# Chunk bounds of a selective attention: from zero-padded blocks on four 64x64 array tiles to full heads on eight 64x32 tiles

## The chip, the cores and the metric

The kernel runs on one core of a Trainium2 chip. The metric is the device time of one execution in microseconds (us); here it is the median of three. A core has five engines with instruction streams of their own: TensorE (PE: matmuls, and PEld: the loading of their weights), VectorE (DVE), ScalarE (ACT), GpSimd (POOL), and SyncE (SP), which only issues transfers here. They work at the same time and wait for each other through semaphores.

## The reference

Two parts, run one after the other: an attention over a selection of chunks, and a gated feed-forward network (FFN).

```python
# q, k, v: 4 batches, 8 heads, 768 positions, 64 dimensions (float32)
chunk, nc, top_k = 32, 24, 6
k_min, k_max = min and max of k over each chunk of 32 positions      # per dimension
ub = sum over d of max(q*k_min, q*k_max)          # bound of each query against each chunk
ub = where(causal by chunks, ub, -1e9)
top_chunks = the 6 chunks of the largest ub, for each query
scores = q @ k.T / 8, kept only in the chosen chunks and not after the query
attn_out = softmax(scores) @ v
x = attn_out as [3072, 512]
xn = x / rms(x) * rms_g
out = (silu(xn @ w_gate) * (xn @ w_val)) @ w_out          # 512 -> 1536 -> 512
```

The change touches `ub` alone. The kernel uses that max(q*k_min, q*k_max) = q*k_min + relu(q)*(k_max - k_min), since k_max is at least k_min: the sum over d becomes two matmuls, q against k_min and relu(q) against the difference.

## The kernel before

One Python program plans the whole kernel: each operation is entered with its engine (or several engines it may go to), a duration, a priority and its dependencies, and a list scheduler fixes the order on every engine before the program is built. So a change of one operation can move all others. TensorE, like the others, then takes its instructions in that fixed order. The sequence is cut into 12 blocks of 256 queries (4 batches by 3), each in two groups `g` of 4 heads; `m` is the block's place in its batch. In the blocks with m = 0 only the last 64 queries need a selection (`w = 64`), as the others see 6 chunks or fewer.

Queries and keys are turned in 32x32 squares, so in `qT` and `kT` the partitions hold 4 heads x 32 dimensions, and the two halves `h` of the 64 dimensions lie side by side in the free dimension. A head's 64 dimensions are then on no common set of 64 partitions. Before, the block `BD` makes up for that: on 64 partitions it has two heads, 32 dimensions each, and its 64 columns belong to one head or the other, with zeros where head and column don't match (`own` is the pattern of ones and zeros). Four matmuls (`t`: two halves of the dimensions, times k_min and difference) add up one bound:

```python
        def upper():
            for k_, g in enumerate(gs):
                qT, qr = sides[i, g][0:2]
                qs = [at(qT)[:, :, BLK - w:], qr()]
                qs = [x.rearrange("p h (j c r) -> p h j c r", c=2, r=CH) for x in qs]
                d = BD[b, g]
                for t in range(4):
                    for hp in range(2):
                        for c in range(2):
                            TE.matmul(bank()[hp][64 * c:64 * (c + 1), k_],
                                      d[64 * hp:64 * (hp + 1), t, :],
                                      qs[t // 2][64 * hp:64 * (hp + 1), t % 2, :, c, :],
                                      start=(t == 0), stop=(t == 3),
                                      skip_group_check=True)

```

Its inputs are made per block and group of heads:

```python
        turn("k")
        half("k")
        for n, op in enumerate((ALU.min, ALU.max)):
            plan.op(f"ext{n}{J}", "DVE", 0.585, 0.67, lambda n=n, op=op: VE.tensor_reduce(
                out=at(kx)[:, n], in_=at(kT).rearrange("p h (c t) -> p h c t", t=CH),
                axis=AXX, op=op), base + 1, reads=[kT], writes=[kx],
                takes=[(kx, "kx")] if n == 0 else ())
        def sub(eng):
            return lambda: eng.tensor_tensor(
                out=at(kx)[:, 1], in0=at(kx)[:, 1], in1=at(kx)[:, 0], op=ALU.subtract)

        first_dk.append(flex(f"dk{J}", {"POOL": (0.175, 0.22, sub(GE)), "DVE": (0.1, 0.16, sub(VE))},
                             base + 2, reads=[kx], writes=[kx]))
        for n in range(2):
            def place(eng, n=n):
                return lambda: eng.tensor_tensor(
                    out=BD[b, g].rearrange("p t (h c) -> p t h c", h=2)[
                        :, 2 * n:2 * n + 2, :, CB * m:CB * (m + 1)],
                    in0=at(kx)[:, n].unsqueeze(2).to_broadcast([P, 2, 2, CB]),
                    in1=own[:].unsqueeze(1).to_broadcast([P, 2, 2, CB]), op=ALU.mult)

            flex(f"bd{n}{J}", {"POOL": (0.21, 0.255, place(GE)), "DVE": (0.11, 0.17, place(VE))},
                 base + 2, reads=[kx, "own", bd], writes=[bd, bd + (m,)])
        turn("q")
        half("q")
        qR = ("qR", *J)

        def qr():
            return at(qraw)[:, g].rearrange("p j h d -> p (j h d)")[:, 0:2 * w].rearrange(
                "p (h s) -> p h s", h=2)

        def relu(eng):
            return lambda: eng.tensor_scalar(
                out=qr(), in0=at(qT)[:, :, BLK - w:], scalar1=HUGE, scalar2=0.0,
                op0=ALU.min, op1=ALU.max)

        flex(f"relu{J}", {"POOL": (0.58 if m else 0.25, 0.62 if m else 0.29, relu(GE)),
                          "DVE": (0.34 if m else 0.14, 0.42 if m else 0.22, relu(VE))},
             base + 2, reads=[qT, qraw], writes=[qR])

        sides[i, g] = (qT, qr, bd, qR, qraw)
```

`turn` is a VectorE transpose, `half` a cast to bf16 for the score matmuls (GpSimd or ScalarE), `flex` an operation that may go to any of the engines named. GpSimd takes `place` or `relu` where the planner finds room there. After `upper`, VectorE turns the bounds back, finds the six largest (`max`), compares and turns the result into masks, which are added to the scores on TensorE.

The FFN's gate works in pieces of 512 columns: two matmul groups into PSUM (`wg`, `wv`), tanh on ScalarE, `tg` on VectorE, and the product `hh` either on GpSimd from a ScalarE copy of the second result (`vs`), or directly on VectorE (the set `DIRECT`). While TensorE would wait in the first 60 us of the plan, dummy matmuls keep it busy (`keep_busy`).

Of the kernel before, what the change touches and what calls it, by code (L numbers as in the profile page):

```python
# [8 lines left out]
FP32 = mybir.dt.float32  # L9
BF16 = mybir.dt.bfloat16  # L10
ALU = mybir.AluOpType
# [103 lines left out]
class Plan:  # L115

    SHARES = ("scale", "relu", "bd0", "bd1", "dk", "mk")
    PATIENT = {"DVE": 0.6}  # L120
    STICK = 60
    RESERVED = ("hh",)
# [188 lines left out]
def kernel(  # L311
# [50 lines left out]
    buffers("VX", 19, [P, 2, 4, D + 1], BF16)  # L362
    buffers("qb", 5, [P, 2, BLK], BF16)
    buffers("kx", 3, [P, 2, 2, CB], FP32)
    buffers("ubn", 1, [P, NG, 2, 4, CH], FP32)
# [18 lines left out]
    pat = sb.tile([P, CH], BF16, name="pat")  # L384
    own = sb.tile([P, 2, CB], FP32, name="own")
    chunkrow = sb.tile([P, S], BF16, name="chunkrow")
# [9 lines left out]
    wo = sb.tile([P, NHT, DM], BF16, name="wo")  # L396
    BD = {(b, g): sb.tile([P, 4, 64], FP32, name=f"BD{b}{g}") for b in range(B) for g in range(NG)}
    TH = DFF // 3
# [5 lines left out]
    assert sorted(ORDER) == [(b, m) for b in range(B) for m in range(NBLK)]  # L404
    PACE, LEAD = 23.0, 60
    MARGIN = 2.0
    FIRST = 8
    FROM = 3
    GATES = {"0": "dk(0, 0, 0)", "1": "dk(0, 0, 0)", "2": "dk(0, 0, 0)", "o": "dk(0, 0, 0)"}
    SPLIT = {0, 1}  # L410
    APART = {0}
    BYDMA = set(range(FROM, len(ORDER)))
    PACKED = {0, 1, 2}
    DIRECT = {(i, hp) for i in range(len(ORDER)) for hp in range(KH) if i >= 8 and hp % 2}

# [3 lines left out]
    def due_attn(i):  # L419
        return PACE * i - LEAD  # L420
# [27 lines left out]
    def constants():  # L448
        def warm():
            SE.activation(out=mhalf[0:1, 0:1], in_=eps6[0:1, 0:1], func=ACT.Exp)  # L450

        plan.op("eps", "POOL", 0.04, 0.1, lambda: GE.memset(eps6[:], 1.0e-6), -400, writes=["eps"])
        plan.op("table", "ACT", 1.4, 1.7, warm, -400, reads=["eps"], writes=["tab"])
        plan.op("half", "POOL", 0.04, 0.12, lambda: GE.memset(mhalf[:], -0.5), -200,
                reads=["tab"], writes=["half"])
        plan.op("ident", "POOL", 0.95, 1.0, lambda: masks.make_identity(nc, ident[:]), -390,
                writes=["ident"])
        plan.op("own", "DVE", 0.2, 0.3, lambda: VE.tensor_reduce(
            out=own[:, :, 0], in_=ident.rearrange("p (x h c) -> p h x c", h=2, c=CH),
            axis=AXXY, op=ALU.add), -380, reads=["ident"], writes=["own0"])  # L460
        plan.op("own8", "DVE", 0.1, 0.2, lambda: VE.tensor_copy(
            own[:, :, 1:CB], own[:, :, 0:1].to_broadcast([P, 2, CB - 1])), -379,
            reads=["own0"], writes=["own0", "own"])
        plan.op("pat", "DVE", 0.2, 0.3, lambda: VE.tensor_reduce(
            out=pat[:], in_=ident.rearrange("p (a c) -> p c a", c=CH), axis=AXX, op=ALU.max),
            -378, reads=["ident"], writes=["pat"])
        plan.op("chunkrow", "DVE", 0.8, 0.9, lambda: VE.tensor_scalar(
            out=chunkrow.rearrange("p (c t) -> p c t", t=CH),
            in0=pat[:, 0:S // CH].unsqueeze(2).to_broadcast([P, S // CH, CH]),
            scalar1=MASKED, scalar2=None, op0=ALU.mult), -300, reads=["pat"], writes=["chunkrow"])  # L470
        for i, (key, t) in enumerate(BD.items()):
            plan.op(f"BD0{key}", "POOL", 0.25, 0.33, lambda t=t: GE.memset(t[:], 0.0), -370 + 42 * i,
                    writes=[("BD", *key)])
        for i, t in enumerate(store["VX"]):
            plan.op(f"ones{i}", "POOL", 0.035, 0.14, lambda t=t: GE.memset(t[:, :, :, D:D + 1], 1.0),
                    -300 + i, writes=[("ones", i)])
# [4 lines left out]

    HELD = {2: (("wg", 1), ("wg", 1)), 3: (("wo", 1), ("wo", 1))}

# [25 lines left out]
    def loads_due(i, n):  # L509
        return -500 + 10 * i + n if i < 2 else due_attn(i) - 20 + n  # L510

# [20 lines left out]

    first_dk = []


    sides = {}

    def pick(i, gs):
# [21 lines left out]
        def upper():  # L560
            for k_, g in enumerate(gs):
                qT, qr = sides[i, g][0:2]
                qs = [at(qT)[:, :, BLK - w:], qr()]
                qs = [x.rearrange("p h (j c r) -> p h j c r", c=2, r=CH) for x in qs]
                d = BD[b, g]
                for t in range(4):
                    for hp in range(2):
                        for c in range(2):
                            TE.matmul(bank()[hp][64 * c:64 * (c + 1), k_],  # L569
                                      d[64 * hp:64 * (hp + 1), t, :],  # L570
                                      qs[t // 2][64 * hp:64 * (hp + 1), t % 2, :, c, :],
                                      start=(t == 0), stop=(t == 3),
                                      skip_group_check=True)

        reads = []
        for g in gs:
            qT, qr, bd, qR, qraw = sides[i, g]
            reads += [bd] + [bd + (x,) for x in range(m + 1)] + [qT, qR, qraw]
        o = plan.op(f"upper{tag}", "PE", (0.925 if m else 0.49) * n, (0.925 if m else 0.49) * n + 0.165,
                    upper, base + 3, reads=reads, writes=ub, takes=[(x, "F") for x in ub])  # L580
# [56 lines left out]
    def job(i, g):  # L637
# [34 lines left out]
        def sub(eng):  # L672
# [4 lines left out]
                             base + 2, reads=[kx], writes=[kx]))  # L677
        for n in range(2):
            def place(eng, n=n):
                return lambda: eng.tensor_tensor(  # L680
                    out=BD[b, g].rearrange("p t (h c) -> p t h c", h=2)[
                        :, 2 * n:2 * n + 2, :, CB * m:CB * (m + 1)],
                    in0=at(kx)[:, n].unsqueeze(2).to_broadcast([P, 2, 2, CB]),
                    in1=own[:].unsqueeze(1).to_broadcast([P, 2, 2, CB]), op=ALU.mult)

            flex(f"bd{n}{J}", {"POOL": (0.21, 0.255, place(GE)), "DVE": (0.11, 0.17, place(VE))},
                 base + 2, reads=[kx, "own", bd], writes=[bd, bd + (m,)])
        turn("q")
        half("q")
        qR = ("qR", *J)  # L690

# [4 lines left out]
        def relu(eng):  # L696
            return lambda: eng.tensor_scalar(  # L697
                out=qr(), in0=at(qT)[:, :, BLK - w:], scalar1=HUGE, scalar2=0.0,
                op0=ALU.min, op1=ALU.max)

        flex(f"relu{J}", {"POOL": (0.58 if m else 0.25, 0.62 if m else 0.29, relu(GE)),
                          "DVE": (0.34 if m else 0.14, 0.42 if m else 0.22, relu(VE))},
             base + 2, reads=[qT, qraw], writes=[qR])

        sides[i, g] = (qT, qr, bd, qR, qraw)
        yield
# [89 lines left out]
        for s in range(2):  # L796
# [13 lines left out]

            pri = base + (-4 if i in SPLIT and not s else 6)
            have = list(pts.values()) + [(pts[x], "ab"[s] if i in SPLIT and x == m else "")
# [95 lines left out]
    def ffn(i):  # L908
# [6 lines left out]
        for toks, h0 in pieces:  # L915
# [10 lines left out]
            for nm, p_, w in (("wg", gp, wg), ("wv", vp, wv)):  # L926
# [11 lines left out]
            plan.op(f"tanh{U}.{hp}", "ACT", 0.48, 0.6, lambda th=th, gp=gp: SE.activation(  # L938
                out=at(th), in_=at(gp), func=ACT.Tanh, scale=0.5), pri - 10, reads=[gp], writes=[th],
                takes=[(th, "th")])  # L940
# [4 lines left out]
            if (i, h0 // 2) in DIRECT:  # L945
                plan.op(f"hh{U}.{hp}", "DVE", 0.6, 0.69, lambda tg=tg, vp=vp, hh=hh: VE.tensor_tensor(
                    out=at(hh), in0=at(tg), in1=at(vp), op=ALU.mult), pri - 60, reads=[tg, vp],
                    writes=[hh], takes=[(hh, "hh")])
                continue
# [3 lines left out]
            plan.op(f"hh{U}.{hp}", "POOL", 1.11, 1.16, lambda tg=tg, vs=vs, hh=hh: GE.tensor_tensor(  # L953
                out=at(hh), in0=at(tg), in1=at(vs), op=ALU.mult), pri - 40, reads=[tg, vs],
                writes=[hh], takes=[(hh, "hh")])
        for s in whole:
# [8 lines left out]
            def project(h0, h1, s=s, op=op, part=part):  # L965
                for ht in range(h0, h1):
# [5 lines left out]
            hhs = sorted({part(ht)[0] for ht in range(last)}, key=str)  # L972
            pri = base + 10 + s
            o = plan.op(f"project{i}.{s}", "PE", 0.216 * last, 0.216 * last + 0.17,
# [4 lines left out]
            o = plan.op(f"project{i}.{s}+", "PE", 0.216 * 2, 0.216 * 2 + 0.17,  # L979
                        lambda project=project: project(last, NHT), pri - 30,  # L980
                        reads=[part(NHT - 1)[0], op], writes=[op])
# [61 lines left out]

    for o in plan.run(in_order=("kraw", "qraw", "vraw", "kT", "qT", "kb", "qb", "VX", "xsT", "xs", "hh", "xnat"),
                      fill=(1.6, 5.6, 60.0, 0.0565, 0.216, "F", keep_busy)):
        o.fn()
# [29 lines left out]
```

## Time and profile before

The three runs took 303.33, 303.45 and 303.48 us; the median is 303.45. The profiled execution has a span of 302.1 us with the TensorE clock granted in full (0.999).

| What | Number | Where |
|---|---|---|
| bound matmuls, line L569 | 768 records, 219 to 320 ns each | groups by line |
| of these, 64x128 and 64x32 | 512 and 256 records | groups by form |
| gate and value matmuls, L931 | 1216 records | groups by line |
| `BD` placement, L680 | 26 on GpSimd, 22 on VectorE | groups by line |
| `mk`, `mtd`, `ubn` (selection) on VectorE | 792, 712, 422 ns for a whole block | groups by form |
| `hh` products, L953 and L946 | 60 on GpSimd at 1197 ns, 12 on VectorE at 688 ns | groups by form |
| DMA | 33.24 MB, mean 110 GB/s | page, part 2 |

The durations of matmul records overlap, since they are pipelined and several array tiles run at once: what a run of matmuls costs is read from the starts in the timeline. The page's slices give busy shares in tenths for 40 equal parts of the span; the stretches give busy us of PE, PEld, DVE, ACT and POOL in a window. A group's row reads: line, engine, operation, output and input, shape, count | busy us, mean ns of one | idle time before it and what ended it.

### The profile page before, as it was taken

To read this page: it belongs to the slowest core of one execution; us is meant where nothing else is said; L and a number is where in the kernel's file an instruction comes from. 1 tells how busy PE (TensorE), PEld (TensorE's weight loads), DVE (VectorE), ACT (ScalarE), POOL (GpSimd) and SP (SyncE) were. 2 spreads that over 40 slices of the span, in tenths; PEclk is the share of its full clock that TensorE was granted. 3 is DMA by queue.
4 is the path that set the end of the run, shared out by engine and by line. 5 is a ranking of instruction groups with operands and counts; after the bars stand their busy time and mean duration, and the time that the engine had idled before them with its cause. 6 is when DMAs were issued, how large, how long until landed. Compare 5 with 4: busy or idle time off the path is not lost.

```text
span 302.1 us, 11334 instructions
## 1 busy us (share of the span) xinstructions
PE 288.5 (96%) x4643; PEld 219.6 (73%) x4668; DVE 220.7 (73%) x564; ACT 213.2 (71%) x371; POOL 162.0 (54%) x273
## 2 busy tenths in 40 slices
PE   8799999999999999999989999999999999999994
PEld 8456786758758858876876788587678588588671
DVE  5997995978897899999999999296254256267250
ACT  3486975879659888987976798568777597554240
POOL 5695675758747684682767578239334044033130
PEclk9999999999999999999999999999999999999999
DMA  7999995758575764666674610101120011020101
GB/s 188 229 201 229 238 215 122 190 117 208 88 167 147 161 142 135 146 110 158 153 159 101 171 37 7 69 4 37 37 69 4 35 53 24 28 61 20 71 0 69
DMA packets 84771, 33.24 MB, mean 110 GB/s; under 512 B 75376, under 2 KB 79984, under 8 KB 84720
## 3 DMA queue, kind: packets, MB, share of 16 engines
q1 hardware_dynamic: 79120, 27.28, 38.5%
q0 software_dynamic: 4752, 4.72, 9.3%
q8 instruction: 36, 0.59, 0.8%
q10 hardware_dynamic: 848, 0.53, 0.7%
q14 instruction: 15, 0.12, 0.1%
HBM read 28.58 MB, written 6.29 MB: 115 GB/s over the span
## 4 chain that ended last, share of the span: by engine, by line
PE 72%; DVE 9%; DMA 7%; ACT 4%; issue 3%; SPq 2%; POOL 1%; ACTq 0%; DVEq 0%; POOLq 0%
PE F L931 33%; PE F L968 18%; PE S L731 6%; PE F L807 6%; PE F L569 5%; DMA wv<-in_moe_w_val_dram 3%; DVE xs L861 3%; DMA qraw<-in_q_dram 2%; PE S L742 2%; SPq L429 2%; DVE tg L942 2%; PE F L1042 1%; DVE kx L668 1%; ACT junk L843 1%; DVE qT L653 1%
## 5 line engine op out<-in xcount | busy, mean ns | idle before, releaser
L781 ACT ACTIVATE pt<-S 128x1024 bf16<-128x1024 f32 (+3 forms) x104 | 87.0, 861 | 17.0 <-PE S L742 16.2
L953 POOL TENSOR_TENSOR hh<-tg,vs 128x512 bf16<-128x512 bf16 x60 | 71.5, 1197 | 45.4 <-ACT vs L950 32.6
L931 PE MATMUL F<-xsT,wg 128*128 128x256 bf16 (+1 forms) x608 | 74.8, 267 | 2.4 <-DVE tg L942 1.9
L931 PE MATMUL F<-xsT,wv 128*128 128x256 bf16 (+1 forms) x608 | 74.7, 267 | 0.9 <-DVE tg L942 0.5
L942 DVE SCALAR_TENSOR_TENSOR tg<-th,F 128x512 bf16<-128x512 bf16 x72 | 48.9, 681 | 31.0 <-ACT th L938 30.2
L968 PE MATMUL F<-wo,hh 128*128 128x512 bf16 x268 | 65.3, 379 | 1.3 <-POOL BD L680 0.2
L931 PEld LDWEIGHTS <-wg 128*128 128x128 bf16 x608 | 55.7, 98 | 10.6 <-issue 3.4
L931 PEld LDWEIGHTS <-wv 128*128 128x128 bf16 x608 | 55.1, 98 | 9.3 <-issue 1.5
L938 ACT ACTIVATE th<-F 128x512 bf16<-128x512 f32 x72 | 43.1, 600 | 20.2 <-PE F L931 19.4
L751 POOL TENSOR_SCALAR_AFFINE_SELECT pt<-pt 128x512 bf16<-128x512 bf16 x48 | 31.5, 661 | 36.9 <-ACT pt L781 36.3
L968 PEld LDWEIGHTS <-hh 128*128 128x128 bf16 x288 | 27.0, 98 | 28.8 <-POOL qraw L697 0.2
L950 ACT ACTIVATE vs<-F 128x512 bf16<-128x512 f32 x60 | 35.7, 603 | 9.1 <-PE F L931 6.5
L731 PE MATMUL S<-qb,kb 32*128 32x256 bf16 (+1 forms) x800 | 33.2, 253 | 1.7 <-ACT qb L660 1.4
L668 DVE TENSOR_REDUCE kx<-kT 128x16 f32<-128x512 f32 x48 | 30.1, 665 | 0.0
L807 PEld LDWEIGHTS <-pt 128*128 128x128 bf16 x672 | 24.8, 98 | 4.8 <-issue 0.8
L807 PE MATMUL F<-VX,pt 128*128 128x65 bf16 x672 | 27.2, 194 | 0.6 <-DVE ubn L599 0.4
L731 PEld LDWEIGHTS <-kb 32*128 32x128 bf16 x800 | 14.2, 92 | 15.0 <-issue 14.1
L861 DVE SCALAR_TENSOR_TENSOR xs<-xnat,ri_all,gB 128x512 bf16<-128x512 bf16 x18 | 21.1, 1212 | 2.7 <-POOL ri_all L851 2.7
L984 ACT ACTIVATE osb<-F 128x512 f32<-128x512 f32 x15 | 8.7, 593 | 18.1 <-PE F L968 18.1
L826 DVE TENSOR_TENSOR xnat<-F,rden 128x256 bf16<-128x256 f32 x48 | 20.0, 423 | 1.2
L742 PE MATMUL S<-mtd,chunkrow 32*128 32x128 bf16 (+2 forms) x384 | 20.8, 203 | 0.0
L742 PE MATMUL S<-mto,chunkrow 32*128 32x128 bf16 (+2 forms) x384 | 20.4, 203 | 0.0
(62 smaller groups left out, 340.2 us busy)
## 6 DMA issues: line engine op xcount, KB each, us to landing
vraw<-in_v_dram SPq DMA_DIRECT2D x24, 256.0 KB, 4.2
out_dram<-osb SPq DMA_DIRECT2D x24, 256.0 KB, 2.3
kraw<-in_k_dram SPq DMA_DIRECT2D x72, 64.0 KB, 2.5
qraw<-in_q_dram SPq DMA_DIRECT2D x72, 64.0 KB, 2.2
wg<-in_moe_w_gate_dram POOLq DMA_DIRECT2D x3, 512.0 KB, 10.1
wv<-in_moe_w_val_dram POOLq DMA_DIRECT2D x3, 512.0 KB, 11.8
wo<-in_moe_w_out_dram POOLq DMA_DIRECT2D x3, 512.0 KB, 20.7
kraw<-in_k_dram SPq DMA_DIRECT2D x10, 128.0 KB, 4.6
```

Of the source, the lines that this page charges most:

```text
L668: plan.op(f"ext{n}{J}", "DVE", 0.585, 0.67, lambda n=n, op=op: VE.tensor_reduce(out=at(kx)[:, n], in_=at(kT).rearrange("p h (c t) -> p h c ...
L731: TE.matmul(s[a // 2][:, a % 2, c0:c0 + q1 - q0], kbt[r, t, ks], qbt[r, t, q0:q1], start=(t == 0), stop=(t == 1 and not mask), skip_group_ ...
L742: TE.matmul(o, chunkrow[r, BLK * kg + P * e:BLK * kg + P * (e + 1)], mv, start=False, stop=(d == 1), skip_group_check=True)
L751: GE.affine_select(out=d, in_=d, compare_op=ALU.is_ge, fill=0.0, base=0, pattern=[[0, 4], [1, P]], channel_multiplier=-1)
L781: lambda pt=pt, hs=hs, c0=c0, c1=c1, x=sc[hp]: SE.activation(out=at(pt)[:, hs, c0:c1], in_=at(x)[:, :, c0:c1], func=ACT.Exp, scale=SCALE), ...
L807: TE.matmul(o[:, a, :], p_[:, a, off:off + P], vt[:, e, a, :], start=(kb_ == 0 and a == 0), stop=(kb_ == nkb - 1 and a == 3), skip_group_c ...
L931: TE.matmul(at(p_)[:, n * W:(n + 1) * W], w[:, g, ht * P:(ht + 1) * P], at(xT)[:, g, x0:x0 + W], start=(g == 0), stop=(g == NP - 1), skip_ ...
L938: plan.op(f"tanh{U}.{hp}", "ACT", 0.48, 0.6, lambda th=th, gp=gp: SE.activation(out=at(th), in_=at(gp), func=ACT.Tanh, scale=0.5), pri - 1 ...
L942: VE.scalar_tensor_tensor(out=at(tg), in0=at(th), scalar=1.0, in1=at(gp), op0=ALU.add, op1=ALU.mult), pri - 20, reads=[th, gp], writes=[tg ...
L950: plan.op(f"vcopy{U}.{hp}", "ACT", 0.48, 0.6, lambda vs=vs, vp=vp: SE.activation(out=at(vs), in_=at(vp), func=ACT.Copy), pri + 0.1, reads= ...
L953: plan.op(f"hh{U}.{hp}", "POOL", 1.11, 1.16, lambda tg=tg, vs=vs, hh=hh: GE.tensor_tensor(out=at(hh), in0=at(tg), in1=at(vs), op=ALU.mult) ...
L968: TE.matmul(at(op)[:], at(key)[:, o:o + P], wo[:, ht, :], start=(ht == 0), stop=(ht == NHT - 1))
```

## The change

Now `BD` is [128, 2, 2, 32] instead of [128, 4, 64]: 64 partitions hold all 64 dimensions of one head, for k_min and the difference (`n_`) and for two heads (`p_`). There are no zeros to multiply. A matmul has 64 rows and 32 columns (24 of them chunks), and the eight of one `n_` go to eight different tiles of the array: 2 row groups (`e`) by 4 column groups. To have the dimensions on the rows, half of each 128 partitions must move by 32: for the bounds by four small VectorE copies after one whole copy; for q by a whole copy into a new float32 buffer `QX` and four copies of 32 partitions each, on VectorE or ScalarE. The relu then reads `QX`. So four matmuls with half zeros become two without, for each head and query half, and the number of matmuls stays the same, as each now serves one head and not two.

The planner's settings change as well: the pace and lead of attention before the FFN (23 to 24, 60 to 67), how long VectorE may wait for a more urgent operation (0.6 to 0.3), how strongly TensorE stays in one tile mode (60 to 25), some priorities; the direct `hh` product is allowed from block 5 on and not 8; blocks 3 and 4 send their FFN input over TensorE instead of a transposing DMA (`FROM`); block 1 selects its two groups of heads apart (`APART`).

```diff
-    SHARES = ("scale", "relu", "bd0", "bd1", "dk", "mk")
-    PATIENT = {"DVE": 0.6}
-    STICK = 60
+    SHARES = ("qx", "qm", "scale", "relu", "bd0", "bd1", "dk", "mk")
+    PATIENT = {"DVE": 0.3}
+    STICK = 25
...
+    buffers("QX", 3, [P, 2, BLK], FP32)
...
-    BD = {(b, g): sb.tile([P, 4, 64], FP32, name=f"BD{b}{g}") for b in range(B) for g in range(NG)}
+    BD = {(b, g): sb.tile([P, 2, 2, 32], FP32, name=f"BD{b}{g}") for b in range(B) for g in range(NG)}
...
-    PACE, LEAD = 23.0, 60
+    PACE, LEAD = 24.0, 67
...
-    FROM = 3
+    FROM = 5
...
-    APART = {0}
+    APART = {0, 1}
...
-    DIRECT = {(i, hp) for i in range(len(ORDER)) for hp in range(KH) if i >= 8 and hp % 2}
+    DIRECT = {(i, hp) for i in range(len(ORDER)) for hp in range(KH) if i >= 5 and hp % 2}
...
+    CROSS = [(0, 32, 0, 1), (64, 96, 0, 1), (32, 0, 1, 0), (96, 64, 1, 0)]
...
-                for t in range(4):
-                    for hp in range(2):
+                for n_ in range(2):
+                    for p_ in range(2):
                         for c in range(2):
-                            TE.matmul(bank()[hp][64 * c:64 * (c + 1), k_],
-                                      d[64 * hp:64 * (hp + 1), t, :],
-                                      qs[t // 2][64 * hp:64 * (hp + 1), t % 2, :, c, :],
-                                      start=(t == 0), stop=(t == 3),
-                                      skip_group_check=True)
+                            for e in range(2):
+                                r = slice(64 * e, 64 * (e + 1))
+                                x = 64 * c + 32 * p_
+                                TE.matmul(bank()[e][x:x + 32, k_], BD[b, g][r, n_, p_, :],
+                                          qs[n_][r, p_, :, c, :], start=(n_ == 0), stop=(n_ == 1),
+                                          skip_group_check=True)
...
-        for n in range(2):
-            def place(eng, n=n):
...
-            flex(f"bd{n}{J}", {"POOL": (0.21, 0.255, place(GE)), "DVE": (0.11, 0.17, place(VE))},
-                 base + 2, reads=[kx, "own", bd], writes=[bd, bd + (m,)])
+        def place(eng):
+            def go():
+                new = BD[b, g][:, :, :, CB * m:CB * (m + 1)]
+                eng.tensor_copy(new, at(kx))
+                for lo, hi, p_, t in CROSS:
+                    VE.tensor_copy(new[hi:hi + 32, :, p_], at(kx)[lo:lo + 32, :, t])
+            return go
+
+        plan.op(f"bd{J}", "DVE", 0.34, 0.4, place(VE), base + 2, reads=[kx, bd], writes=[bd, bd + (m,)])
...
+        flex(f"qx{J}", {"DVE": (0.34 if m else 0.14, 0.42 if m else 0.22, spread(VE)),
+                        "POOL": (0.58 if m else 0.25, 0.62 if m else 0.29, spread(GE)),
+                        "ACT": (0.54 if m else 0.24, 0.63 if m else 0.33, spread(SE))},
+             base + 2, reads=[qT], writes=[qx], takes=[(qx, "QX")])
+        for n in range(2):
+            def move(eng, n=n):
+                def go():
+                    for lo, hi, p_, t in CROSS[2 * n:2 * n + 2]:
+                        o, x = at(qx)[hi:hi + 32, p_, BLK - w:], at(qT)[lo:lo + 32, t, BLK - w:]
+                        if eng is SE:
+                            SE.activation(out=o, in_=x, func=ACT.Copy)
+                        else:
+                            eng.tensor_copy(o, x)
+                return go
+
+            flex(f"qm{n}{J}", {"DVE": (0.39 if m else 0.19, 0.47 if m else 0.27, move(VE)),
+                               "ACT": (0.8 if m else 0.54, 0.9 if m else 0.62, move(SE))},
+                 base + 2, reads=[qT, qx], writes=[qx + (n,)])
...
         def relu(eng):
             return lambda: eng.tensor_scalar(
-                out=qr(), in0=at(qT)[:, :, BLK - w:], scalar1=HUGE, scalar2=0.0,
+                out=qr(), in0=at(qx)[:, :, BLK - w:], scalar1=HUGE, scalar2=0.0,
```

`SHARES` lists how the names of those VectorE operations begin that the planner keeps apart in time from GpSimd's. The new operation is named `bd(...)`, which no entry matches.

## The prediction

> **What bounds the kernel now.** I read the page's busy shares first, then its slices. Each digit of a slice is a tenth of 7.6 us.
>
> ```profile
> PE 288.5 (96%) x4643; PEld 219.6 (73%) x4668; DVE 220.7 (73%) x564; ACT 213.2 (71%) x371; POOL 162.0 (54%) x273
> ...
> PE   8799999999999999999989999999999999999994
> ...
> DVE  5997995978897899999999999296254256267250
> ACT  3486975879659888987976798568777597554240
> ```
>
> TensorE is near full from the third slice on. That alone isn't proof, because up to 60 us the kernel fills waiting time with dummy matmuls (41 of 128x512 and 86 of 128x128 by the table of groups), and they count as busy. So I asked for the stretches after 60 us: columns are stretch, length, then busy us of PE, PEld, DVE, ACT, POOL.
>
> ```profile
> 100.00:120.00 20.00, 19.57 (x363) 14.79 (x364) 19.22 (x68) 17.24 (x29) 12.59 (x22) 1.00 0.62 140
> 120.00:140.00 20.00, 19.79 (x333) 14.98 (x334) 18.58 (x52) 17.11 (x30) 11.59 (x17) 1.00 0.58 117
> 140.00:160.00 20.00, 18.92 (x374) 16.12 (x370) 19.37 (x51) 17.10 (x30) 14.29 (x22) 1.00 0.70 167
> 160.00:180.00 20.00, 19.65 (x384) 15.17 (x387) 19.35 (x67) 15.72 (x27) 13.40 (x23) 1.00 0.46 108
> ...
> 240.00:260.00 20.00, 19.89 (x356) 16.12 (x356) 10.66 (x19) 15.62 (x25) 7.12 (x9) 1.00 0.15 42
> ```
>
> Two things are to be seen. PE is the bound everywhere after 60 us, with about 2 us idle in 100 to 180. But in those 80 us VectorE has only 80 - 76.5 = 3.5 us left: it is a second bound lying right under the first. After 200 us (attention over, only the FFN left) VectorE is half free.
>
> Next, the matmuls that change, line L569, in the timeline of one group with 256 queries (start, length, count):
>
> ```profile
> 97.05 0.67 PE L569 MATMUL F<-qT,BD 64*64 64x128 f32 x16
> 97.54 0.62 PE L569 MATMUL F<-qraw,BD 64*64 64x128 f32 x16
> 97.97 0.62 PE L569 MATMUL F<-qT,BD 64*64 64x128 f32 x16
> 98.41 0.62 PE L569 MATMUL F<-qraw,BD 64*64 64x128 f32 x16
> 98.96 1.07 PE L807 MATMUL F<-VX,pt 128*128 128x65 bf16 x28
> ```
>
> Starts, not lengths, give the cost: 98.96 - 97.05 = 1.91 us for 64 records. A float32 matmul leaves two records, so these are the 32 matmuls of two head groups. Sixteen records take 0.43 us, and on 4 tiles that is 4 per tile at 108 ns each. The small groups (64 queries) take 1.07 us:
>
> ```profile
> 63.28 0.43 PE L569 MATMUL F<-qT,BD 64*64 64x32 f32 x16
> ...
> 64.35 0.62 PE L887 MATMUL F<-ident,xs 128*128 128x128 bf16 x8
> ```
>
> There are 8 large groups and the equivalent of 4 small ones: 8 x 1.91 + 4 x 1.07 = 19.6 us of TensorE in all.
>
> [...] 108 ns per record and tile with no gap. No run here shows 8 yet. [...] placing the bounds (L680) on VectorE takes 143 ns at best, 179 in the median, and 1030 at worst. [...] The one-source relu here (128x512, three on VectorE) averages 574 ns with a median over both sizes of 412[...].
>
> **The change part by part.**
>
> *TensorE.* The number of matmuls stays (384), and so does what each streams. What changes is that eight run at once. 64 records on 8 tiles are 8 per tile x 108 ns = 0.86, plus the ramp of the first sixteen (0.49 against 0.43) and some tail: 0.95 us against 1.91. Over 8 large groups that saves 8 x 0.95 = **7.6 us**, all after 60 us, where PE is the bound. A small group should come to 0.5 to 0.6 us, but three of the four stand before 60 us, where dummy matmuls still take up slack; I count **0.5 us**. The instruction order of the changed program (built, not timed) has 16 more TensorE transposes, as two more blocks take that way to the FFN instead of a DMA: eight of them take 0.55 us on the chain, so +**1.1 us**. It has 126 stretches of tile mode against 122, which I leave at zero. Sum on TensorE: -7.0 us.
>
> *VectorE.* Gone: 22 placements (22 x 298 ns = 6.6), 4 differences (4 x 435 = 1.7), 4 weighted scalings (4 x 1212 = 4.8), the `own` pattern (1.7). New: 24 copies of 128x32 and 96 of 32x16 into BD. No row of before has such copies; a memset of 64x16 takes 72 ns, so I estimate 75 to 100 ns: 24 x 0.1 + 96 x 0.075 = 9.6. Then 16 q moves at some 0.2 and 6 at 0.1 (3.8), five more relus (+2.0), 9 more direct products `hh` (9 x 688 = 6.2), 7 more output evictions (7 x 682 = 4.8), 1.5 of smaller pieces. Net 27.9 - 14.8 = **+13 us**[...].
>
> ```profile
> L680 DVE TENSOR_TENSOR BD<-kx,own 128x32 f32<-128x32 f32 x22 | 5.8, 298 | 0.0
> ...
> L673 DVE TENSOR_TENSOR kx<-kx 128x16 f32<-128x16 f32 x7 | 3.0, 435 | 0.0
> ...
> L628 ACT ACTIVATE mto<-mtd 64x256 bf16<-64x256 bf16 x5 | 2.1, 416 | 3.0 <-DVE mtd L618 2.9
> ...
> L628 ACT ACTIVATE mto<-mtd 64x64 bf16<-64x64 bf16 x1 | 0.3, 255 | 0.0
> ```
>
> *ScalarE.* It gets 74 of the 96 q moves. The nearest rows are the `mto` copies above: 48 x 416 + 26 x 255 = 26.6 us, plus 8 whole-q copies (about 4.7), 4 scalings and 8 evictions of transposed x (6.3). It loses 9 `vs`, 7 `osb`, 15 casts and 2 V casts at 593 to 643 ns (19.2). Net **+18 us**, to some 77% of the span; in 100 to 180 us it was 84% busy.
>
> *GpSimd.* It loses 26 placements (6.8) and 9 products (9 x 1197 = 10.8), and gains 13 casts (8.7) and 16 whole-q copies (7.6): about -2 us.
>
> *On the path.* VectorE had 3.5 us left in 100 to 180. The part of its new work that belongs to attention (BD, moves and relus less placements and differences) is 9.6 + 3.8 + 2.0 - 8.3 = 7 us over 24 jobs, about 4 of it in that stretch, plus part of the direct products. FFN work can slide to the half-empty end, but TensorE takes its matmuls in a fixed order, so a late selection stops it. I add **+2 us** of new TensorE waits there. 303.45 - 7.0 + 2.0 gives **298.4 us**.
>
> **Rivals.** (1) *TensorE gain in full*: the order was replanned (pace 24, lead 67, attention further ahead), and VectorE's added work falls where it has room, in the first 60 us (80% busy) and after 200. For it: PE hardly waits for VectorE today (2.4 us for `tg` in all). It makes 295 to 297. (2) *VectorE becomes the bound*: the new BD copies come five in a row[...], and the placements already average twice their best case. If each set of five loses 0.3 to 0.4 us, that is 8 us more, and the whole gain is gone: 302 to 305. Against it: `dk` moves to GpSimd and the copies are short. (3) *Eight tiles don't run at twice four*: weight loads or issue set a floor. For it: the small group takes 1.07 us although its stream is a quarter, so something else than streaming already costs 67 ns per matmul and tile. Against it: its weights halve too, 64 to 32 columns. If a large group only reaches 1.3 us, the gain falls to 4.9 us, and the time to about 301. (4) *ScalarE holds up the exponentials*, whose S buffers gate the score matmuls: 1 to 3 us; its 16% of slack speaks against more.
>
> **Range and chances.** Rivals 1 and 2 span 295 to 305; I hold full success and partial loss about equally likely, total loss less so, as the plan was retuned around the new loads. 80% range 293.5 to 303.5. The 2% line lies at 297.4, just under my centre: faster 0.42, same 0.52, slower 0.06.
>
> **What would show it.** In the profile after: a large group of L569's successor with 64 records in 0.95 us between starts (right), or 1.3 and more (rival 3). PE busy down by about 7 us, DVE up to about 234 to 240, ACT to about 230. BD copies near 75 to 100 ns (right) or several hundred (rival 2). PE idle in 60 to 200 us, 2.9 us now, at 5 to 6 (right), under 4 (rival 1), or over 9 with VectorE as releaser (rival 2). The prediction would fail if the retimed order, and not the costs listed, moved the time: for instance a later start of the FFN, or a longer tail after 280 us.

## The result, and the profile after

The changed kernel takes 329.26 us against 303.47 us: slower by a factor of 1.0856 (95% interval 1.0818 to 1.0893). The prediction was 298.4 us, with 293.5 to 303.5 as its range. So it was wrong, and by far.

First the page of the changed kernel: the engines' busy time, then the slices (the last row is the granted TensorE clock in tenths).

```profile
PE 297.6 (91%) x4681; PEld 220.5 (67%) x4681; DVE 259.2 (79%) x702; ACT 232.0 (71%) x434; POOL 159.0 (48%) x268
...
PE   8798858989699899699979989899999999999995
...
DVE  6979996497989999989999999998985436427361
...
PEclk9879997997969999879999999999999999999999
```

ScalarE gained 18.8 us and GpSimd lost 3.0, as predicted (18 and -2). VectorE gained 38.5 us where 13 were expected, or some 19 at most (a busy time of up to 240 us). Its stretch of nines now lasts until about 220 us, and TensorE has gaps all through it. The granted TensorE clock, full before (0.999), drops in several slices of the first half, in one to 0.6.

The stretches show the same. The first fence is after; columns as before: stretch, length, busy us of PE, PEld, DVE, ACT, POOL, then the granted clock.

```profile
100.00:120.00 20.00, 18.13 (x295) 13.26 (x294) 19.17 (x72) 16.94 (x32) 12.97 (x20) 1.00 0.42 104
120.00:140.00 20.00, 17.00 (x265) 12.07 (x263) 19.52 (x42) 17.92 (x33) 14.03 (x24) 0.93 0.43 91
140.00:160.00 20.00, 20.00 (x346) 15.48 (x345) 18.73 (x56) 17.25 (x33) 14.28 (x19) 0.90 0.63 145
160.00:180.00 20.00, 17.82 (x416) 13.87 (x400) 19.27 (x75) 15.30 (x27) 8.25 (x13) 1.00 0.61 127
180.00:200.00 20.00, 18.03 (x277) 13.20 (x276) 19.30 (x43) 16.25 (x29) 12.01 (x21) 1.00 0.46 112
```

VectorE is as full as before in 100 to 180 us, and stays so in 180 to 220 as well, where it was two thirds busy at 180 to 200. Of the first 80 us here, TensorE is idle for 7 and not 2. Over the whole stretch 60 to 200 us, one row of each kernel, before and then after:

```profile
60.00:200.00 140.00, 137.12 (x2454) 105.47 (x2463) 123.03 (x363) 111.18 (x190) 87.91 (x139) 1.00 0.54 123
```

```profile
60.00:200.00 140.00, 125.78 (x2023) 91.46 (x2021) 129.47 (x367) 111.43 (x207) 83.06 (x128) 0.94 0.49 115
```

TensorE idles 14.2 us instead of 2.9 and gets through 2023 records instead of 2454. The prediction had set "over 9 with VectorE as releaser" as the sign of its second rival. The releasers, from the view of TensorE's waits (us in total, times, longest):

```profile
PE F L949 <- DVE tg L960: 3.6, 4, 2.0
PE F L949 <- DVE xnat L844: 2.8, 1, 2.8
PE F L825 <- DVE xsT L918: 2.6, 1, 2.6
PE F L905 <- DVE tg L960: 2.2, 1, 2.2
PE F L566 <- DVE BD L678: 2.1, 5, 1.1
```

These are the five with the largest totals. All are VectorE's, but four are not the changed operations: it looks as if VectorE were late as a whole, and with it whatever stands next in its queue. The chain that ended last agrees. Its shares of the span by engine, before and then after:

```profile
PE 72%; DVE 9%; DMA 7%; ACT 4%; issue 3%; SPq 2%; POOL 1%; ACTq 0%; DVEq 0%; POOLq 0%
```

```profile
PE 43%; DVE 35%; DMA 11%; issue 4%; SPq 3%; POOL 2%; ACT 1%; DVEq 0%; ACTq 0%; POOLq 0%
```

What made it late should show in VectorE's groups, where new rows stand (count | busy us, mean ns):

```profile
L678 DVE COPY BD<-kx 32x16 f32<-32x16 f32 x96 | 28.8, 300 | 1.9
...
L703 DVE COPY QX<-qT 32x256 f32<-32x256 f32 x16 | 5.7, 354 | 0.3
L676 DVE COPY BD<-kx 128x32 f32<-128x32 f32 x24 | 5.2, 219 | 0.2
L703 DVE COPY QX<-qT 32x64 f32<-32x64 f32 x6 | 2.9, 482 | 0.1
```

A copy of 16 elements per partition takes 300 ns in the mean, and the 120 bound copies take 34.0 us where 9.6 were estimated. The line's own view gives minimum, median and maximum:

```profile
L678 DVE COPY BD<-kx x96: 161/169/1336, 11.5 to 224.5; 32x16 f32<-32x16 f32 x96
```

So two things are too dear: the floor of 161 ns, twice the estimate, and a tail up to 1336. One place in the timeline shows both. VectorE, then GpSimd (start us, length us):

```profile
107.91 0.14 DVE L676 COPY BD<-kx 128x32 f32<-128x32 f32 x1
108.08 1.82 DVE L678 COPY BD<-kx 32x16 f32<-32x16 f32 x4
109.93 0.59 DVE L676 COPY BD<-kx 128x32 f32<-128x32 f32 x1
110.55 0.70 DVE L678 COPY BD<-kx 32x16 f32<-32x16 f32 x4
```

```profile
108.11 0.61 POOL L656 CAST qb<-qT 128x512 bf16<-128x512 f32 x1 [0.45 <-DVE BD L676]
108.67 0.62 POOL L689 COPY QX<-qT 128x512 f32<-128x512 f32 x1
109.26 0.61 POOL L715 TENSOR_SCALAR qraw<-QX 128x512 f32<-128x512 f32 x1
109.84 0.65 POOL L769 TENSOR_SCALAR_AFFINE_SELECT pt<-pt 128x512 bf16<-128x512 bf16 x1
111.27 0.64 POOL L769 TENSOR_SCALAR_AFFINE_SELECT pt<-pt 128x512 bf16<-128x512 bf16 x1 [0.79 <-ACT pt L799]
```

While GpSimd works without a break (108.1 to 110.5), four copies need 1.82 us. Record by record, the first takes 165 ns and the next three 495, 542 and 578, and each of these three ends 21 to 27 ns after one of GpSimd's operations does. In the pause that follows, four need 0.70. Of the 96 copies, 31 took over 200 ns. All of these began while a GpSimd operation ran (as did 14 of the other 65), and 28 of them ended within 40 ns after the end of one.

The part that the change was made for did come. A large group of bound matmuls, 64 records, in TensorE's timeline:

```profile
238.99 0.45 PE L566 MATMUL F<-QX,BD 64*32 64x128 f32 x16
239.23 0.42 PE L566 MATMUL F<-qraw,BD 64*32 64x128 f32 x16
239.45 0.48 PE L566 MATMUL F<-QX,BD 64*32 64x128 f32 x16
239.67 0.52 PE L566 MATMUL F<-qraw,BD 64*32 64x128 f32 x16
240.13 2.12 PE L986 MATMUL F<-wo,hh 128*128 128x512 bf16 x9
```

Sixteen records start every 0.22 us and not every 0.43: eight tiles do run at twice four. The group takes 240.13 - 238.99 = 1.14 us against 1.91. Six of the eight large groups ran without a break: five at the full clock, in 1.09 to 1.44 us (the longest with a wait of 0.24 behind it), and one in 1.61 us, mostly at a granted clock of 0.50. The small group (64 queries) that ran whole at the full clock took 0.84 us against 1.07.

### The profile page after: what moved, and what is told of

It reads as the page before. It is cut to its first block, busy times and chain, and to the rows that moved or that the text cites. A ratio compares the mean times of both kernels' runs of the same rounds, so it can differ in the third digit from the quotient of the medians.

```text
span 328.4 us, 11559 instructions
## 1 busy us (share of the span) xinstructions
PE 297.6 (91%) x4681; PEld 220.5 (67%) x4681; DVE 259.2 (79%) x702; ACT 232.0 (71%) x434; POOL 159.0 (48%) x268
## 4 chain that ended last, share of the span: by engine, by line
PE 43%; DVE 35%; DMA 11%; issue 4%; SPq 3%; POOL 2%; ACT 1%; DVEq 0%; ACTq 0%; POOLq 0%
PE F L949 23%; PE F L986 10%; DVE kx L663 6%; DVE BD L678 5%; DMA kraw<-in_k_dram 4%; DMA vraw<-in_v_dram 4%; DVE tg L960 4%; PE F L825 4%; DVE qT L648 3%; SPq L429 3%; PE S L749 3%; DVE kT L648 3%; PE F L566 2%; DVE xnat L844 2%; DVE m L603 1%
## 5 line engine op out<-in xcount | busy, mean ns | idle before, releaser
L971 POOL TENSOR_TENSOR hh<-tg,vs 128x512 bf16<-128x512 bf16 x51 | 60.2, 1182 | 66.7 <-ACT vs L968 35.7
L949 PE MATMUL F<-xsT,wg 128*128 128x256 bf16 (+1 forms) x608 | 78.2, 275 | 9.9 <-DVE tg L960 3.4
L949 PE MATMUL F<-xsT,wv 128*128 128x256 bf16 (+1 forms) x608 | 77.4, 273 | 0.2 <-DVE tg L960 0.2
L960 DVE SCALAR_TENSOR_TENSOR tg<-th,F 128x512 bf16<-128x512 bf16 x72 | 48.4, 678 | 25.8 <-ACT th L956 25.2
L986 PE MATMUL F<-wo,hh 128*128 128x512 bf16 x288 | 68.7, 384 | 0.0
L949 PEld LDWEIGHTS <-wv 128*128 128x128 bf16 x608 | 57.0, 100 | 8.5 <-issue 0.8
L968 ACT ACTIVATE vs<-F 128x512 bf16<-128x512 f32 x51 | 30.4, 601 | 8.0 <-PE F L949 6.9
L678 DVE COPY BD<-kx 32x16 f32<-32x16 f32 x96 | 28.8, 300 | 1.9
L701 ACT ACTIVATE QX<-qT 32x256 f32<-32x256 f32 (+1 forms) x74 | 26.5, 358 | 2.5 <-POOL QX L689 1.3
L1004 DVE TENSOR_SCALAR osb<-F 128x512 f32<-128x512 f32 x16 | 10.8, 681 | 15.6 <-PE F L986 15.5
L861 ACT ACTIVATE junk<-xnat 128x512 bf16<-128x512 bf16 x24 | 15.1, 628 | 11.1 <-DVE xnat L844 10.8
```

The source lines that it names most:

```text
L678: VE.tensor_copy(new[hi:hi + 32, :, p_], at(kx)[lo:lo + 32, :, t])
L949: TE.matmul(at(p_)[:, n * W:(n + 1) * W], w[:, g, ht * P:(ht + 1) * P], at(xT)[:, g, x0:x0 + W], start=(g == 0), stop=(g == NP - 1), skip_ ...
L960: VE.scalar_tensor_tensor(out=at(tg), in0=at(th), scalar=1.0, in1=at(gp), op0=ALU.add, op1=ALU.mult), pri - 20, reads=[th, gp], writes=[tg ...
L968: plan.op(f"vcopy{U}.{hp}", "ACT", 0.48, 0.6, lambda vs=vs, vp=vp: SE.activation(out=at(vs), in_=at(vp), func=ACT.Copy), pri + 0.1, reads= ...
L986: TE.matmul(at(op)[:], at(key)[:, o:o + P], wo[:, ht, :], start=(ht == 0), stop=(ht == NHT - 1))
```

## The experiments

All times are medians beside runs of the kernel before on the same chip (303.35 to 303.80 us). The theories: **A**, the small VectorE copies of the bounds; **B**, the planner's new settings; **C**, the moves of q.

### What the bound copies cost, and why

**Left out.** The order on all engines is the changed kernel's, less the 96 copies.

```diff
-                for lo, hi, p_, t in CROSS:
-                    VE.tensor_copy(new[hi:hi + 32, :, p_], at(kx)[lo:lo + 32, :, t])
```

> The changed kernel with its 96 small copies of bounds across partitions left out (half of the bounds are then not in place); the order on all engines is otherwise that of the changed kernel. Theory A (these VectorE copies, 28.8 us busy in the profile after, make VectorE late and TensorE wait in its fixed order): VectorE busy falls from 259 to about 230 us and the time to 297 to 306 us. Theory B (the new settings of the planner make a worse order): it stays above 318 us. Theory C (the q moves on ScalarE hold it up): it stays above 318 us too.

Measured: 302.10 us, ratio 0.9949 (0.9931 to 0.9966); VectorE busy 231.0. The 96 copies account for 329.26 - 302.10 = 27.2 us, more than the whole loss of 25.8: without them the kernel is slightly faster than before. Theory A holds; B and C can't carry the loss.

**As reductions.** Same data, shapes and order, another kind of operation. The question is whether waits for GpSimd make the copies' mean of 300 ns, and whether this kind has them as well:

```diff
-                    VE.tensor_copy(new[hi:hi + 32, :, p_], at(kx)[lo:lo + 32, :, t])
+                    VE.tensor_reduce(out=new[hi:hi + 32, :, p_], in_=at(kx)[lo:lo + 32, :, t].unsqueeze(3),
+                                     axis=AXX, op=ALU.max)
```

> The 96 copies are written as reductions over an axis of one element: same data, same shapes, same order[...]. [...] it falls to 160 to 180 ns, VectorE busy falls by about 12 us, and the time to 308 to 320 us. If the 300 ns belong to the copies themselves, mean and time stay (328 us).

Measured: 313.67 us, ratio 1.0334 (1.0295 to 1.0374). The line's view in this run:

```profile
L678 DVE TENSOR_REDUCE BD<-kx x96: 156/160/166, 11.4 to 206.5; 32x16 f32<-32x16 f32 x96
```

The tail is gone: 166 ns at most, where the copy reached 1336. So the copies waited for GpSimd's operations and the same moves written as reductions did not, though GpSimd was no less busy (87.1 us in 60 to 200, against 83.1). Why the one kind waits is not shown. These waits are worth 329.26 - 313.67 = 15.6 us. But 160 ns stay, and so do 10 us over the kernel before.

**One set of partitions, first try.** All four copies read partitions 0 to 31 and write 32 to 63; half of the bounds are then missing.

```diff
-                    VE.tensor_copy(new[hi:hi + 32, :, p_], at(kx)[lo:lo + 32, :, t])
+                    VE.tensor_copy(new[32:64, :, p_], at(kx)[0:32, :, t])
```

> The four copies of a set all read partitions 0 to 31 and write 32 to 63 (half of the bounds are then wrong or missing); number, shape and order as in the changed kernel. If a copy is held until the one before has finished because it begins in another set of 32 partitions, the starts of undisturbed copies come 80 to 100 ns apart and not 170, VectorE gains 5 to 7 us and the time falls by 4 to 10 us, to about 320. If the 170 ns are the price of any small copy, nothing changes (328 us).

Measured: 323.85 us, ratio 1.0663 (1.0634 to 1.0692); an undisturbed set takes 0.64 us, not 0.70. Record by record, its starts lie 198, 84 and 192 ns apart, against 178, 180 and 176 in the changed kernel. The first two copies now write the same place, and so do the last two: there the wait is longer. Only the middle step has neither a change of partitions nor a common place, and it is the short one: there a copy begins before the last one has ended, since it takes 156 ns at least. So one step of three is free of that wait, but the time mixes both effects.

**One set of partitions, second try.** As reductions, and into four separate places of a scratch tile:

```diff
-                for lo, hi, p_, t in CROSS:
-                    VE.tensor_copy(new[hi:hi + 32, :, p_], at(kx)[lo:lo + 32, :, t])
+                for x, (lo, hi, p_, t) in enumerate(CROSS):
+                    VE.tensor_reduce(out=scr[32:64, x], in_=at(kx)[0:32, :, t].unsqueeze(3), axis=AXX, op=ALU.max)
```

> As the run with the copies written as reductions (313.7 us, four in 0.68 to 0.70 us), but all four read partitions 0 to 31 and write four different places of a scratch tile on partitions 32 to 63 (half of the bounds are then missing). Held by a change of partitions: four take 0.40 us, starts about 80 ns apart, VectorE loses 7 us and the time falls to 305 to 310 us. If the price belongs to each small operation, nothing changes.

Measured: 304.54 us, ratio 1.0024 (1.0011 to 1.0037), just under the range. A set in the timeline, first with the true partitions (the run with reductions), then with one set of partitions:

```profile
42.18 0.68 DVE L678 TENSOR_REDUCE BD<-kx 32x16 f32<-32x16 f32 x4
```

```profile
41.01 0.39 DVE L679 TENSOR_REDUCE scr<-kx 32x16 f32<-32x16 f32 x4
```

The last of the four starts (0.39 - 0.15)/3 = 80 ns after the one before, against (0.68 - 0.16)/3 = 173. The same number of operations of the same kind and size costs half when they all begin on the same partitions. With changing partitions each begins some 13 ns after the last one has ended (173 against 160 ns of duration; 13 to 32 ns in the records of the changed kernel), on the same partitions 69 ns before that (80 against 149). This later start is worth 313.67 - 304.54 = 9.1 us of the kernel's time, and the 96 operations themselves only 304.54 - 302.10 = 2.4. The scratch run also frees the bound matmuls from waiting for the four operations, but that is little: in the run with reductions only weight loads waited for them, 0.9 us in all.

**No move at all.** Besides the bound copies, the q moves are left out (`CROSS[2 * n:2 * n + 2]` becomes an empty tuple); the whole copies into `QX` and `BD` stay.

> Without the 96 bound copies and without the 96 q moves (q and the bounds are then not all in place); the rest in the same order. Theory A: within 4 us of the run without the bound copies alone. Theory C: 8 us or more below it. Either way it shows what the eight-tile matmuls are worth when nothing is moved for them: I expect 293 to 300 us, TensorE's gain of 7 us in full.

Measured: 296.72 us, ratio 0.9793 (0.9747 to 0.9838). The q moves are worth 5.4 us: more than theory A wanted, less than C. And eight tiles with nothing moved for them would gain 6.6 us, the new settings included. Taken in this order, the steps are (in another order each might weigh differently):

| Step | us | Change |
|---|---|---|
| kernel before, these runs | 303.35 | |
| eight tiles and settings, nothing moved | 296.72 | -6.6 |
| q moved by copies | 302.10 | +5.4 |
| 96 small reductions, all on the same partitions | 304.54 | +2.4 |
| begun on changing partitions | 313.67 | +9.1 |
| as copies, which waited for GpSimd | 329.26 | +15.6 |

The scratch run stood beside runs of the kernel before at 303.80 us and not 303.35; by its ratio it would be 304.1 here, which moves some 0.5 us from the line of the 96 reductions to the line of the changing partitions.

The clock belongs to these terms. It was 0.958 in the changed kernel's profile (0.958 to 0.972 over its four runs) and 0.994 to 1.000 in the profiles of the four runs between. The run with reductions has the same matmul records in the same order, and its page says:

```profile
PE 287.4 (92%) x4681; PEld 214.8 (69%) x4681; DVE 246.9 (79%) x702; ACT 231.5 (75%) x434; POOL 158.6 (51%) x268
```

With copies TensorE was busy for 297.6 us. Of the 17.6 us between the two profiled spans (328.4 and 310.8), 10.2 are thus the same matmuls taking longer, and 7.4 more idle time of TensorE. In the changed kernel the granted clock was 0.50 in five stretches, 27.2 us together, in which TensorE was busy for 23.9 us; at the full clock that work would take about 12 (an estimate, 23.9 x 0.50). A gate matmul of 128x256 took 414 to 421 ns in two of these stretches, and 273 at the full clock. So the lower clock can account for the 10.2, and a good part of the 15.6 us came by way of the clock. Why the clock fell is not shown. TensorE's idle time alone hardly explains it: in 60 to 200 us it idled 12.3 us in the run with reductions, at a clock of 1.00, and 14.2 in the changed kernel, at 0.94.

### The settings and the booking

**New settings on the old method.** The kernel before with the changed pace, lead, patience, tile-mode preference, priorities, `FROM`, `APART` and `DIRECT`, and two smaller entries on when inputs and weights are loaded.

> The kernel before with the new settings of the planner alone (pace, lead, patience, tile mode, priorities, direct products from block 5, the DMA way from block 5, two groups apart in block 1); the zero blocks stay. Theory A (moves cost the time) gives 300 to 308 us, near the kernel before. Theory B (the settings cost it) gives 315 us or more.

Measured: 306.41 us, ratio 1.0099 (1.0065 to 1.0134). Theory B explains 2.8 us, not 26. **The old settings on the new method:**

> The changed kernel's method with the planner's settings of before. Theory A: no better than the changed kernel, 322 to 340 us, VectorE busy above 250 us, the bound copies at 250 to 350 ns again. Theory B: back to 300 to 308 us.

Measured: 329.70 us, ratio 1.0879 (1.0842 to 1.0915): the loss doesn't depend on them.

**Telling the planner.** It booked 0.34 us for a set of five copies that takes 34.0/24 = 1.42 us in the mean, and kept nothing apart, as the operation's name matched no entry of `SHARES`.

```diff
-    SHARES = ("qx", "qm", "scale", "relu", "bd0", "bd1", "dk", "mk")
+    SHARES = ("qx", "qm", "scale", "relu", "bd", "dk", "mk")
...
-        plan.op(f"bd{J}", "DVE", 0.34, 0.4, place(VE), base + 2, reads=[kx, bd], writes=[bd, bd + (m,)])
+        plan.op(f"bd{J}", "DVE", 0.87, 0.93, place(VE), base + 2, reads=[kx, bd], writes=[bd, bd + (m,)])
```

> The changed kernel, but the planner books 0.87 us for a set of five bound copies and not 0.34, and keeps them apart from GpSimd's operations. If the wrong booking (an order that doesn't fit what VectorE can do) is a large part of the loss beside the work itself, the copies' mean falls to 170 to 220 ns and the time to 305 to 316 us. If the work alone counts, it stays at 320 us or more.

Measured: 322.96 us, ratio 1.0601 (1.0542 to 1.0660). The copies' mean stayed at 267 ns with a maximum of 1208, so in the run they were not kept apart from GpSimd's operations: this shows what the booking is worth, not what a real separation would be. And the reductions, booked at 0.85 us a set:

> The copies as reductions and booked with their true 0.85 us a set, new settings. Against 313.7 us with the same work booked at 0.34: if the wrong booking costs on top of the work, 304 to 310 us; if not, 312 to 316 us.

Measured: 311.87 us, ratio 1.0268 (1.0238 to 1.0299), against 313.67 with the wrong booking. The booking misled whoever planned this, but a true one wins back only 2 to 6 us: the rest is the work itself, with its waits.

### What TensorE's gain is worth

**Half the bound matmuls, no moves.** The kernel before in its own order, with two of four matmuls left out, so half of each bound is missing.

```diff
-                for t in range(4):
+                for t in (0, 2):
...
-                                      start=(t == 0), stop=(t == 3),
+                                      start=(t == 0), stop=(t == 2),
```

> The kernel before with two of its four bound matmuls left out (half of the dimensions or heads are missing), everything else and the order as before: TensorE's part of the gain with no move and no new setting. If TensorE is the bound it takes all 7 to 10 us: 294 to 297 us. If VectorE lies close under it, only 3 to 5 us: 298 to 301 us.

Measured: 299.46 us, ratio 0.9853 (0.9834 to 0.9873), 4.3 us less. A large group took 1.04 us in its timeline, 0.87 less than before: 8 x 0.87 = 7.0 us less TensorE work after 60 us. Only some 60% of that reached the end. What keeps the rest? Two runs took work off VectorE, with the reductions over one position of each chunk instead of 32:

```diff
-                out=at(kx)[:, n], in_=at(kT).rearrange("p h (c t) -> p h c t", t=CH),
+                out=at(kx)[:, n], in_=at(kT).rearrange("p h (c t) -> p h c t", t=CH)[:, :, :, 0:1],
```

> The kernel before, but its 48 chunk reductions on VectorE read one position of each chunk and not 32 (the bounds are then those of one position); all orders as before. VectorE loses about 24 us of busy time, TensorE nothing. If TensorE alone sets the time, 302 to 304 us. If VectorE is a bound too, 297 to 301 us.

> Both: the light reductions and half of the bound matmuls left out, all orders as before. The half alone gave 299.5 us. If VectorE was what kept the rest of TensorE's gain back, the two gains add up to more than their sum or at least to all of TensorE's work, 7 to 8 us below the run with light reductions alone. If something else did (the fixed order, ScalarE), the step is again only about 4 us.

Measured: 302.00 us (0.9947, 0.9929 to 0.9966) with light reductions alone, and 296.23 (0.9768, 0.9741 to 0.9795) with both. Taking 22.6 us off VectorE (198.1 busy against 220.7) alone gives 1.4 us: TensorE is the first bound of the kernel before. With VectorE light, the half of the matmuls is worth 5.8 us and not 4.3, which lies between the two expectations (7 to 8, or 4). So VectorE kept back about 1.5 us, give or take 1.2 by the intervals; the last 1.2 of the 7.0 stays open.

### Attempts at a better version

**GpSimd moves.** The bound copies go to GpSimd, and the q moves may:

```diff
-        plan.op(f"bd{J}", "DVE", 0.34, 0.4, place(VE), base + 2, reads=[kx, bd], writes=[bd, bd + (m,)])
+        plan.op(f"bd{J}", "POOL", 1.0, 1.05, place(GE), base + 2, reads=[kx, bd], writes=[bd, bd + (m,)])
...
-            flex(f"qm{n}{J}", {"DVE": (0.39 if m else 0.19, 0.47 if m else 0.27, move(VE)),
+            flex(f"qm{n}{J}", {"POOL": (0.7 if m else 0.4, 0.75 if m else 0.45, move(GE)),
+                               "DVE": (0.39 if m else 0.19, 0.47 if m else 0.27, move(VE)),
```

(and the four small copies use `eng` instead of `VE`)

> The whole set of bound copies on GpSimd (booked 1.0 us), and the q moves allowed there too. GpSimd is 48% busy in the changed kernel, VectorE the bound: theory A gives VectorE busy near 225 us and a time of 298 to 306 us, if a small GpSimd copy takes 250 ns or less. If it takes 400 ns or more, GpSimd itself becomes late (over 70% busy) and the time stays over 310 us.

Measured: 306.71 us, ratio 1.0109 (1.0077 to 1.0142). VectorE is down to 230.1 us, and GpSimd's copies are even, as their row shows:

```profile
L678 POOL COPY BD<-kx x96: 186/192/378, 15.1 to 194.8; 32x16 f32<-32x16 f32 x96
```

That wins back 22.6 of the 25.8 us. It ends 0.7 us above the range that was expected, and only reaches the old method at the same settings (306.41).

**One set for both groups of heads.** `kx` and `BD` hold both groups, so a block needs one set of five copies on GpSimd and not two (13 sets in all, with 52 small copies); `qm` may go to GpSimd, booked at 0.86; some settings were chosen anew (`PACE` 23.5, `LEAD` 75, `APART` {0}, two priorities). `STICK` stayed at 25 in the kernel that ran, where the expectation says 60.

> A version meant to be better: the bound copies of both groups of heads in one set of five on GpSimd (48 small copies and not 96), the difference too, q moves allowed on GpSimd, all booked with measured durations, settings chosen anew for these (tile mode 60, lead 75, one block apart). GpSimd's share falls against the run with two sets (306.7 us), VectorE stays near 228 us: I expect 299 to 304 us.

Measured: 305.95 us, ratio 1.0065 (1.0043 to 1.0087): a miss. What keeps the gain back here was not tested; the bound copies are off VectorE and about half as many, and the q moves remain, which cost 5.4 us in their first form, against a gain of 6.6 at best. No version here beats the kernel before; the runs below it all leave work out.

## Why the prediction was wrong

- **TensorE.** The mechanism was right, the size a little high: about 1.1 us for a large group where 0.95 was worked out, so 8 x 0.8 = 6.4 us and not 7.6. The first sixteen and the tail cost more than "some tail". A small group took 0.84 us where 0.5 to 0.6 was said. Counting the gain in full on the path was the second slip: alone, 7.0 us of it gave 4.3.
- **VectorE: the step that failed.** "I estimate 75 to 100 ns: 24 x 0.1 + 96 x 0.075 = 9.6" measured 34.0 us. Of the 28.8 us of the 96 small copies, 15.4 remained when they were written as reductions; the other 13.4 are waits for GpSimd's operations, all but a little: the 31 copies of over 200 ns were 12.8 us longer than at the median. The memset that the estimate was taken from (72 ns) has no input to read. The profile before had operations that do: 143 ns at best for the `BD` placement, 151 for the difference, 155 in the mean for a `max` over 8 elements. The 161 (copy) and 156 ns (reduction) at best here are close to these, and not to the memset; the prediction, which quotes the 143, still priced by the memset. Those `max` operations do start about 75 ns apart in a row (16 in 1.27 us), which makes small operations look cheap; the scratch run has such spacing too (80 ns), the one that changes partitions has not (173).
- **The q moves** on VectorE were 8.6 us, not 3.8, with means of 354 and 482 ns; on ScalarE 414 and 254 ns, as the rows chosen had said. Against this, the weighted scalings on VectorE fell by 8.8 us and not 4.8, since the 14 that stayed were also shorter (921 ns in the mean, 1212 before). With the 24.4 us too little for the bound copies and 4.8 for the q moves, this explains nearly all of 38.5 instead of 13.
- **The path.** "+2 us" should have been about 32, and part of that is not waiting but the lower clock (0.958), which the prediction took as full throughout. The reading before it was right: VectorE had 3.5 us left in 100 to 180, and TensorE's fixed order turned lateness into waits (14.2 us idle in 60 to 200, against 2.9). But the 4 us that the prediction itself put into that stretch, before any direct product, were already more than what was left there.
- **Rival 2** named the culprit (the bound copies, five in a row) and the sign in the profile, but sized it at 0.3 to 0.4 us a set. A set took 1.42 against 0.4 in the estimate, so 1.0 us more. It lacked the later start on changing partitions and the floor of 161 ns; and three of the four copies of one set waited for GpSimd in turn (495, 542 and 578 ns).
- **Rival 3** was wrong: no floor from weight loads or issue shows at 128 columns (0.22 us for sixteen records, 0.43 before). Only in the small group, whose 0.84 us is far more than a quarter of 1.14, does something else than the stream set the time. **Rival 4**: TensorE's score matmuls waited 1.5 us for ScalarE's exponentials (0.3 before), within its 1 to 3 us.
- **The retimed order**, the last worry, costs 2.8 us by itself, on the old method.
- **Slips in the sums**, none of which matters: the 22 placements kept VectorE busy for 5.8 us (the row's figure, in which overlapping ones count once), not 6.6; ScalarE's "15 casts" already hold the two of V; GpSimd's items give -1.3 and not -2.

## What to carry to other kernels

Price a small VectorE operation by a row that reads an input and changes partitions the same way, and by starts in a row, not by a memset (72 ns here, where the copies took 161 at best). Before adding such operations to an engine that has only a few per cent left, compare the whole addition with what is left in that stretch. When a layout must move data by 32 partitions, count the instructions: four per set at 160 ns or more outweighed halving the matmuls' time here. Written as a reduction over an axis of one, such a copy had no waits for GpSimd (166 ns at most, where the copy reached 1336).

## What the runs showed that was not expected

- A start on other partitions than the last operation's doubled the spacing of the small VectorE reductions: 173 ns against 80.
- VectorE and GpSimd took turns operation by operation in one place: four copies of 16 elements took 1.82 us between GpSimd operations of 0.6 us, and 0.70 without.
- The granted TensorE clock was 0.50 in five stretches of the changed kernel, one of them 6.8 us from 89.4 on, though no single wait of TensorE or its weight loads in the list is longer than 2.9 us. TensorE's own matmuls took longer there (a gate matmul of 128x256 414 to 421 ns in two of them, against 273): against the reductions, the copies cost 7.4 us in idle time of TensorE and 10.2 in its busy time.
- GpSimd moved 16 elements by 32 partitions in 192 ns in the median and 378 at most, without VectorE's tail (1336).
